# Two small transfers of 64 query weight rows, over eight DMA engines, for the second and third group

## The chip, the core and the metric

The kernel runs on one core of a Trainium2 chip. The metric is the time of one execution on the device in microseconds, the median of several runs. A profile is one further execution with the hardware profiler on; its rows are quoted as the profile prints them.

## The reference

One decode step of a block with attention over cached keys and values and an MLP, for 4 sequences, in float32:

```python
# B=4, D=448, 16 query heads on 8 key heads, Dh=256, window W=1024 of the cache
q = layernorm(x) @ wq                        # wq: 448 x 4096
scores = einsum("bhqd,bhkd->bhqk", q, k[-W:]) * Dh ** -0.5
o = einsum("bhqk,bhkd->bhqd", softmax(scores), v[-W:])
h = x + o @ wo                               # wo: 4096 x 448
y = layernorm(h)
out = h + gelu(y @ w1 + b1) @ w2 + b2        # F = 1792
```

About 88 MB of keys, values and weights are read once. The work per byte is small.

## The kernel before, in words

**Groups.** The 8 key heads are 8 groups, 0 to 7. A group has two query heads and needs its part of the query weights wq (448 rows x 512 columns), keys, values and a part of wo. For each group TensorE projects the queries (`project_q`, line 152, with a transposition at 158), multiplies them with the keys in two halves (`scores_half`, line 172), transposes the probabilities (line 204), multiplies with the values (`values`, line 216) and adds the group's share of the output (`add_output`, line 245). VectorE takes maxima, scales and copies; ScalarE copies and takes exponentials. The MLP follows at the end, with w1 at line 443 and w2 at lines 469 (`pa`) and 479 (`py`).

**Loads.** All loads are issued by the sync engine SP, in the order of the program, through `load` (line 58) into three ring slots of 128 rows (tag `r`). Slot `t0` takes wq of group 0 with x and biases (`wq0`) and then the keys of group 0 with the first 384 rows of group 1's wq (`k0`). Four kinds of ring load follow, twice: `ta` (from `la`), `tb` (`lb`), `tc` (`lc`) and `td` (`ld`), for three groups each time, 14080 or 15872 words a row. The last loads go into the slots `te`: keys and values of the last groups, w1 and w2. w2 comes in four pieces, the last of which has 448 words a row. A ring slot is loaded again as soon as its readers are done; SP waits for them. The order on TensorE, ScalarE and SP is that of the program text.

**The query weights.** 448 is three times 128 and a rest of 64 rows. `wq_parts` (line 70) lists a group's products. Rows 0 to 383 are three products of 128 rows x 512 columns. The rest is usually packed on the host as 128 rows x 256 columns, the left half of the columns above the right half, and needs two products of 256 columns: `yT[:, 3]` has the normalised x in its upper 64 rows and zeros below, `yT[:, 4]` the other way round. Group 1 is the exception: its rest comes as plain 64 rows x 512 columns in a small tile of its own, `wq1_last`, and is one product. That tile is loaded by two transfers at line 265, between `k0` and the first ring load. Their source has an outer dimension of 8, with a gap of 512 words behind each eighth, and each fills 32 rows of the tile.

In the names of the views `wq_last<-wq` is that small load, `pq` a projection, `s` scores, `po` the product with the values. `yT`, `project_q(g, ...)` and the loop `for g in (0, 3)`, which handles groups g+1 to g+3, are what the change touches.

Of the kernel before, what the change touches and what calls it, by code (L numbers as in the profile page):

```python
# [8 lines left out]
F32 = mybir.dt.float32  # L9
# [6 lines left out]
B, D = 4, 448  # L16
HQ, HKV, SK, DH = 16, 8, 4096, 256
# [3 lines left out]
P = 128  # L21
H = P // 2
# [4 lines left out]
Q = 32  # L27
CACHE = NKC * B * DH
HALF = CACHE // 2
WEIGHTS = 4 * D  # L30
# [3 lines left out]
SCALE = DH ** -0.5  # L34

@with_exitstack
def block_kernel(ctx: ExitStack, tc, wq0, k0, wq1, la, lb, lc, ld, k7, vo, w1, w2, out):
    nc = tc.nc
    const = ctx.enter_context(tc.tile_pool(name="const", bufs=1))
    ring = ctx.enter_context(tc.tile_pool(name="ring", bufs=3))  # L40
    work = ctx.enter_context(tc.tile_pool(name="work", bufs=2))
# [9 lines left out]
    def slot(name):  # L51
        return ring.tile([P, SLOT], F32, tag="r", name=name)

    def load(t, at, src, pieces=None):
        dst = t[:, at : at + src.shape[-1]]
        at = 0
        for n in pieces or (src.shape[-1],):
            nc.sync.dma_start(dst[:, at : at + n], src[:, at : at + n])  # L58
            at += n
        return dst  # L60

    def cut(t, sizes):
        parts, at = [], 0
        for n in sizes:
            parts.append(t[:, at : at + n])
            at += n
        return parts


    def wq_parts(t, last=None):  # L70
        parts = [(a, yT[:, a, :], slice(0, 512), t[:, a * 512 : (a + 1) * 512]) for a in range(3)]
        if last is not None:
            return parts + [(3, yT[:H, 3, :], slice(0, 512), last)]
        for i in range(2):
            parts.append((3, yT[:, 3 + i, :], slice(i * 2 * P, (i + 1) * 2 * P), t[:, 3 * 512 :]))
        return parts


    def keys(t):
        return t.rearrange("p (c b k) -> p c b k", c=2, b=B)  # L80

    def chunks(t):
        v = t.rearrange("p (c b d) -> p c b d", b=B, d=DH)
        return [v[:, c : c + 2] for c in range(0, v.shape[1], 2)]
# [17 lines left out]

    yT = const.tile([P, ND + 1, Q], F32, name="yT")
    nc.vector.memset(yT, 0.0)
    wq1_last = const.tile([H, 512], F32, name="wq1_last")
    zT = const.tile([P, ND, Q], F32, name="zT")
    nc.vector.memset(zT, 0.0)

# [40 lines left out]
    def project_q(g, parts):  # L149
        pq = ps_m.tile([P, 512], F32, tag="m", name=f"pq{g}")  # L150
        for j, y, cols, w in parts:
            nc.tensor.matmul(pq[j * Q : (j + 1) * Q, cols], y, w, start=True, stop=True)  # L152
        qs = work.tile([P, 512], F32, tag="qs", name=f"qs{g}")
        nc.scalar.copy(qs, pq)  # L154

        pt = ps_m.tile([P, 2 * REP, P], F32, tag="m", name=f"pqt{g}")
        for i in range(2 * REP):
            nc.tensor.transpose(pt[:, i, :], qs[:, i * P : (i + 1) * P], ident)  # L158
        sm = work.tile([P, 2 * REP, B], F32, tag="sm", name=f"sm{g}")
        nc.vector.tensor_reduce(  # L160
            sm, pt.rearrange("p i (j q) -> p i q j", j=4)[:, :, :B, :], axis=AX.X, op=ALU.add
        )

        src = sm.rearrange("p (r c) b -> p c b r", r=REP)
        for i in range(2):
            nc.vector.tensor_copy(qT[g % 2][:, :, :, i * REP : (i + 1) * REP], src)
# [13 lines left out]
    def softmax(g, parts):  # L180
        halves, mx = zip(*parts)
        nm = work.tile([P, 1], F32, tag="nm", name=f"nm{g}")
        nc.vector.tensor_max(nm, mx[0], mx[1])
        nc.vector.tensor_scalar_mul(nm, nm, -SCALE)  # L184
        p = once.tile([P, 2 * 512], F32, tag="p", name=f"p{g}")
        sums = work.tile([P, 2], F32, tag="sums", name=f"sums{g}")
        for h in range(2):
            nc.scalar.activation(  # L188
                p[:, h * 512 : (h + 1) * 512], halves[h], AF.Exp, bias=nm, scale=SCALE,
                accum_out=sums[:, h : h + 1],  # L190
            )
        rec = work.tile([P, 1], F32, tag=f"rec{g % 3}", name=f"rec{g}")
        nc.vector.tensor_add(rec, sums[:, 0:1], sums[:, 1:2])
        nc.vector.reciprocal(rec, rec)
        return p, rec

    def scores(g, kt):
        return [scores_half(g, h, kt[h]) for h in range(2)]

    def transpose_p(g, p):  # L200
        for h in range(2):
            pt = ps_t.tile([P, 4, P], F32, tag="t", name=f"ppt{g}_{h}")
            for c in range(4):
                nc.tensor.transpose(pt[:, c, :], p[:, (4 * h + c) * P : (4 * h + c + 1) * P], ident)  # L204

            src = pt.rearrange("p (c i) (b q) -> p c i b q", i=2, b=B)
            for i in range(2):
                nc.vector.tensor_copy(  # L208
                    pT[g % 2][:, 2 * h : 2 * h + 2, :, i * REP : (i + 1) * REP], src[:, :, i, :, :REP]
                )  # L210


    def values(g, vt, po, pairs=range(NKC // 2)):
        for c in pairs:
            for b in range(B):
                nc.tensor.matmul(  # L216
                    po[b * Q : (b + 1) * Q], pT[g % 2][:, c, b, :], vt[c][:, :, b, :],
                    start=(c == 0), stop=(c == NKC // 2 - 1),
                )
# [35 lines left out]
    def po_tile(g, pool=ps_o, tag="o"):  # L255
        return pool.tile([P, 2, DH], F32, tag=tag, name=f"po{g}")


    t = slot("t0")
    wqt, xT, b2T, b1T = cut(load(t, 0, wq0), (WEIGHTS, ND * B, 4, 4 * 4))  # L260
    wqt = wq_parts(wqt)
    xT = xT.rearrange("p (a b) -> p a b", a=ND)
    ka, kb, wqt1 = cut(load(t, WEIGHTS + COLUMNS, k0), (HALF, HALF, 3 * 512))
    for i in range(2):
        nc.sync.dma_start(  # L265
            wq1_last[i * Q : (i + 1) * Q, :], wq1[i].rearrange("e (p c) -> e p c", c=512)[:, :4, :]
        )
    d = work.tile([P, ND, B], F32, tag="d", name="d_x")
    centred(d, xT, "x")
    sx = work.tile([P, ND, B], F32, tag="sx", name="sx")  # L270
# [20 lines left out]
        nc.scalar.copy(rs[:, at : at + cols], pr.rearrange("p i c -> p (i c)")[:, :cols])  # L291

    parts = scores(0, [keys(ka), keys(kb)])
    project_q(1, wq_parts(wqt1, wq1_last))
    p, rec = softmax(0, parts)
    transpose_p(0, p)

    def finish(g, po, rec, wt):
        transposed_output(g, po, rec)
        add_output(g, output_weights(wt))  # L300

    for g in (0, 3):
        ka, kb, wqt, va = cut(load(slot(f"ta{g}"), 0, la[g // 3]), (HALF, HALF, WEIGHTS, HALF))
        parts = scores(g + 1, [keys(ka), keys(kb)])
        project_q(g + 2, wq_parts(wqt))
        p, rec_next = softmax(g + 1, parts)
        transpose_p(g + 1, p)
        po = po_tile(g)
        va = chunks(va)
        values(g, va, po, range(0, 2))  # L310

        vb, wot, ka, kb = cut(load(slot(f"tb{g}"), 0, lb[g // 3]), (HALF, WEIGHTS, HALF, HALF))
        values(g, va + chunks(vb), po, range(2, 4))
        p, rec_then = softmax(g + 2, scores(g + 2, [keys(ka), keys(kb)]))
        finish(g, po, rec, wot)
        transpose_p(g + 2, p)

        wqt, v, wot, ka = cut(load(slot(f"tc{g}"), 0, lc[g // 3]), (WEIGHTS, CACHE, WEIGHTS, HALF))
        project_q(g + 3, wq_parts(wqt))
        po = po_tile(g + 1)  # L320
        values(g + 1, chunks(v), po)
        first_half = scores_half(g + 3, 0, keys(ka))
        finish(g + 1, po, rec_next, wot)

        kb, wqt, v, wot = cut(load(slot(f"td{g}"), 0, ld[g // 3]), (HALF, WEIGHTS, CACHE, WEIGHTS))
        parts = [first_half, scores_half(g + 3, 1, keys(kb))]
        project_q(g + 4, wq_parts(wqt))
        p, rec = softmax(g + 3, parts)
        transpose_p(g + 3, p)
        po = po_tile(g + 2)  # L330
        values(g + 2, chunks(v), po)
        finish(g + 2, po, rec_then, wot)


    g = HKV - 2
    e = [slot(f"te{i}") for i in range(3)]
# [7 lines left out]
    p, rec_last = softmax(g + 1, scores(g + 1, kt))  # L344
# [27 lines left out]
    last = ps_s.tile([P, 512], F32, tag="s", name="last")[:, :P]  # L372
# [102 lines left out]
    for c in range(first, NFC):  # L475
        for j in range(4):
            m, n = (Q, 2) if c == first else (B, 2 if j < 3 else 1)
# [79 lines left out]
```

## Time and profile before

| | |
|---|---|
| median of 3 runs | 213.85 us (213.79 to 213.94) |
| profiled execution | 214.16 us |
| its span, first to last instruction | 212.4 us |
| DMA engines, queue of the loads | 96.9% of 16 engines' span |
| TensorE busy | 133.9 us (63%) |
| VectorE, ScalarE busy | 39.0 us, 22.1 us |
| read from HBM | 88.23 MB |

A line of the busy list gives engine, busy time, share of the span and number of instructions. In rows of groups and of the timeline stand line, engine, operation and tiles, written from read, and in brackets how long the engine had been idle and what ended that. SP's rows are the issues of transfers. In rows of stretches stand start and end, length, busy time of PE (matmul), PEld (weight load), DVE (VectorE), ACT (ScalarE) and POOL (GpSimd), each with its number of instructions, then the clock granted to TensorE, the mean share of the 16 DMA engines that is busy, and GB/s. A DMA row of a queue has packets, MB and share. The chain of waits is followed back from the last instruction.

### The profile page before, as it was taken

Reading aid. Unit: us, or ns where it says so; the run is one execution under the profiler, and the core shown is the slowest. Engines: PE = TensorE matmul, PEld = TensorE weight load, DVE = VectorE, ACT = ScalarE, POOL = GpSimd, SP = SyncE. Lnnn points to the kernel's source line nnn. Section 1 sums busy time; section 2 is a strip of 40 time slices with the busy share of each in tenths; the row PEclk is TensorE's granted clock in tenths of the full one; section 3 lists DMA queues with packets and bytes.
Section 4 is the critical chain, followed back from the end, with each engine's and each line's share of the span. In section 5 each row is a group of like instructions: output and inputs, shape, how many; then the busy total and the mean of one; then the engine's idle time right before and its main releaser. Section 6 shows DMA issues by size and latency. Waiting matters only on the chain.

```text
span 212.4 us, 2302 instructions
## 1 busy us (share of the span) xinstructions
PE 133.9 (63%) x976; PEld 48.3 (23%) x976; DVE 39.0 (18%) x170; ACT 22.1 (10%) x54; POOL 5.0 (2%) x16
## 2 busy tenths in 40 slices
PE   0469805843950696288398098138708879978984
PEld 0342201310220221022123023013202323224432
DVE  1520300410230003022013013100301223112310
ACT  2011300300020100030003002001000302010311
POOL 5100000000000000000000000000000000000200
PEclk9999995995896559589969759856985999999999
DMA  7999898999999999999999999999989999999991
GB/s 294 425 396 534 361 488 361 491 394 475 407 395 529 395 407 430 451 403 459 424 424 488 403 395 505 395 430 419 478 350 460 430 429 394 440 400 444 419 384 52
DMA packets 3257, 88.43 MB, mean 416 GB/s; under 512 B 368, under 2 KB 624, under 8 KB 1328
## 3 DMA queue, kind: packets, MB, share of 16 engines
q1 hardware_dynamic: 3248, 88.30, 96.9%
q8 instruction: 7, 0.11, 0.2%
q14 instruction: 2, 0.02, 0.0%
HBM read 88.23 MB, written 0.07 MB: 416 GB/s over the span
## 4 chain that ended last, share of the span: by engine, by line
DMA 78%; PE 16%; SPq 2%; DVE 1%; issue 1%; ACT 1%; ACTq 0%
DMA tb<-lb 22%; DMA ta<-la 21%; DMA td<-ld 20%; DMA te<-w 14%; PE s L172 6%; PE po L216 4%; SPq L58 2%; PE ppt L204 1%; PE pq L152 1%; PE acc L245 1%; PE pa L469 1%; PE py L479 1%; SPq L265 1%; PE pqt L158 1%; ACT qs L154 1%
## 5 line engine op out<-in xcount | busy, mean ns | idle before, releaser
L177 DVE TENSOR_REDUCE mx<-s 128x1 f32<-128x512 f32 x16 | 11.1, 691 | 57.8 <-PE s L172 57.8
L172 PE MATMUL s<-ta,qT 128*32 128x512 f32 x64 | 10.7, 831 | 10.3 <-DMA ta<-la 10.3
L154 ACT COPY qs<-pq 128x512 f32<-128x512 f32 x8 | 4.7, 585 | 113.3 <-PE pq L152 113.3
L188 ACT ACTIVATE p<-s,nm 128x512 f32<-128x512 f32 x16 | 10.9, 687 | 46.1 <-DVE nm L184 46.1
L233 DVE TENSOR_SCALAR o<-po,rec 128x512 f32<-128x512 f32 x8 | 6.0, 750 | 48.5 <-PE po L216 48.5
L216 PE MATMUL po<-tb,pT 128*32 128x512 f32 x32 | 7.2, 1051 | 12.2 <-DMA tb<-lb 12.2
L172 PE MATMUL s<-td,qT 128*32 128x512 f32 x32 | 7.1, 1042 | 12.1 <-DMA td<-ld 12.1
L152 PE MATMUL pq<-tc,yT 128*32 128x512 f32 (+1 forms) x20 | 3.9, 891 | 16.6 <-DMA tc<-lc 16.6
L204 PE MATMUL ppt<-ident,p 128*128 128x128 f32 x64 | 10.5, 287 | 0.7 <-ACT p L188 0.4
L216 PE MATMUL po<-tc,pT 128*32 128x512 f32 x64 | 10.4, 813 | 0.0
L158 PE MATMUL pqt<-ident,qs 128*128 128x128 f32 x32 | 6.6, 341 | 6.0 <-ACT qs L154 6.0
L204 PEld LDWEIGHTS ppt<-ident,p 128*128 128x128 f32 x64 | 6.7, 141 | 6.3 <-ACT p L188 6.3
L160 DVE TENSOR_REDUCE sm<-pqt 128x16 f32<-128x64 f32 x8 | 1.8, 224 | 34.4 <-PE pqt L158 34.4
L216 PE MATMUL po<-te,pT 128*32 128x512 f32 x64 | 7.5, 595 | 0.5 <-DMA te<-vo 0.5
L172 PE MATMUL s<-tb,qT 128*32 128x512 f32 x64 | 7.4, 607 | 0.0
L216 PE MATMUL po<-td,pT 128*32 128x512 f32 x64 | 7.3, 595 | 0.0
L237 PE MATMUL pot<-ident,o 128*128 128x128 f32 x32 | 5.2, 286 | 2.7 <-DVE o L233 2.7
L158 PEld LDWEIGHTS pqt<-ident,qs 128*128 128x128 f32 x32 | 4.2, 169 | 11.4 <-ACT qs L154 9.7
L351 PE MATMUL warm<-idle 128*32 128x512 bf16 x22 | 6.8, 382 | 0.0
L172 PEld LDWEIGHTS s<-ta,qT 128*32 128x32 f32 x64 | 2.6, 148 | 17.7 <-issue 13.7
L208 DVE COPY pT<-ppt 128x16 f32<-128x16 f32 x32 | 4.7, 171 | 7.6 <-PE ppt L204 7.6
L172 PE MATMUL s<-t,qT 128*32 128x512 f32 x32 | 5.4, 833 | 0.5 <-DMA t<-k 0.5
(134 smaller groups left out, 112.4 us busy)
## 6 DMA issues: line engine op xcount, KB each, us to landing
tc<-lc SPq DMA_DIRECT2D x2, 7936.0 KB, 47.0
td<-ld SPq DMA_DIRECT2D x2, 7936.0 KB, 44.0
ta<-la SPq DMA_DIRECT2D x2, 7040.0 KB, 38.1
tb<-lb SPq DMA_DIRECT2D x2, 7040.0 KB, 43.2
te<-vo SPq DMA_DIRECT2D x1, 4992.0 KB, 28.1
t<-k SPq DMA_DIRECT2D x1, 4864.0 KB, 15.8
te<-k SPq DMA_DIRECT2D x1, 4096.0 KB, 37.8
te<-vo SPq DMA_DIRECT2D x1, 3072.0 KB, 14.8
```

The source lines that it names most:

```text
L152: nc.tensor.matmul(pq[j * Q : (j + 1) * Q, cols], y, w, start=True, stop=True)
L154: nc.scalar.copy(qs, pq)
L158: nc.tensor.transpose(pt[:, i, :], qs[:, i * P : (i + 1) * P], ident)
L172: nc.tensor.matmul(s[b * Q : (b + 1) * Q, :], qT[g % 2][:, c, b, :], kt[:, c, b, :], start=(c == 0), stop=(c == 1),)
L177: nc.vector.reduce_max(m, s, axis=AX.X)
L188: nc.scalar.activation(p[:, h * 512 : (h + 1) * 512], halves[h], AF.Exp, bias=nm, scale=SCALE, accum_out=sums[:, h : h + 1],)
L204: nc.tensor.transpose(pt[:, c, :], p[:, (4 * h + c) * P : (4 * h + c + 1) * P], ident)
L208: nc.vector.tensor_copy(pT[g % 2][:, 2 * h : 2 * h + 2, :, i * REP : (i + 1) * REP], src[:, :, i, :, :REP])
L216: nc.tensor.matmul(po[b * Q : (b + 1) * Q], pT[g % 2][:, c, b, :], vt[c][:, :, b, :], start=(c == 0), stop=(c == NKC // 2 - 1),)
L233: nc.vector.tensor_scalar_mul(o, po, rec)
L237: nc.tensor.transpose(pt[:, i, c], o[:, i, c * P : (c + 1) * P], ident)
L351: nc.tensor.matmul(warm[:Q], idle[:, :Q], idle, start=True, stop=True)
```

## The change

The tile `wq1_last` (64 rows) becomes `wq_last` (128 rows): group 1's rest lies in rows 0 to 63, group 2's in rows 64 to 127. The two transfers stand at the same place in SP's order, and each now brings 64 rows of 512 words. The source again has an outer dimension of 8 and a gap behind each eighth. The first ring load no longer holds group 2's rest and has 256 words a row less; for that `la` becomes two tensors, `la0` and `la1`. Group 2's projection has one product of 64 rows x 512 columns, with `yT[H:, 4]` as its other side. Groups 3 to 7 are as before.

```diff
-    wq1_last = const.tile([H, 512], F32, name="wq1_last")
+    wq_last = const.tile([P, 512], F32, name="wq_last")
...
     for i in range(2):
-        nc.sync.dma_start(
-            wq1_last[i * Q : (i + 1) * Q, :], wq1[i].rearrange("e (p c) -> e p c", c=512)[:, :4, :]
-        )
+        nc.sync.dma_start(wq_last[i * H : (i + 1) * H], wq_rest[i].rearrange("e (p c) -> e p c", c=512)[:, :8, :])
...
         if last is not None:
-            return parts + [(3, yT[:H, 3, :], slice(0, 512), last)]
+            return parts + [(3, last[0], slice(0, 512), last[1])]
...
-    project_q(1, wq_parts(wqt1, wq1_last))
+    project_q(1, wq_parts(wqt1, (yT[:H, 3, :], wq_last[:H])))
...
     for g in (0, 3):
-        ka, kb, wqt, va = cut(load(slot(f"ta{g}"), 0, la[g // 3]), (HALF, HALF, WEIGHTS, HALF))
+        n = WEIGHTS if g else 3 * 512
+        ka, kb, wqt, va = cut(load(slot(f"ta{g}"), 0, la[g // 3]), (HALF, HALF, n, HALF))
         parts = scores(g + 1, [keys(ka), keys(kb)])
-        project_q(g + 2, wq_parts(wqt))
+        project_q(g + 2, wq_parts(wqt, None if g else (yT[H:, 4, :], wq_last[H:])))
...
-    la = np.concatenate([k[1:5:3], wq[2:6:3], va[0:4:3]], axis=2)
+    la0 = np.concatenate([k[1], wq[2][:, : 3 * 512], va[0]], axis=1)
+    la1 = np.concatenate([k[4], wq[5], va[3]], axis=1)
...
-    wq1 = np.asarray(A_wq).reshape(D, HKV, 512)[3 * P :, 1].reshape(2, 8, 4 * 512)
-    wq1 = np.concatenate([wq1, np.zeros((2, 8, 512), np.float32)], axis=2)
+    wq_rest = np.asarray(A_wq).reshape(D, HKV, 512)[3 * P :, 1:3].transpose(1, 0, 2).reshape(2, 8, 8 * 512)
+    wq_rest = np.concatenate([wq_rest, np.zeros((2, 8, 512), np.float32)], axis=2)
```

On SP's queue at the start of the program the transfers stood like this (written from read, rows x words):

```order
L58 DMA t_129<-wq 128x1828
L58 DMA t_129<-k 128x9728
L265 DMA wq_last<-wq 32x1x512 x2
L58 DMA ta_247<-la 128x14080
L58 DMA tb_321<-lb 128x14080
L58 DMA tc_390<-lc 128x15872
```

Now they are these:

```order
L59 DMA t_129<-wq 128x1828
L59 DMA t_129<-k 128x9728
L266 DMA wq_last<-wq_rest 64x1x512 x2
L59 DMA ta_247<-la 128x13824
L59 DMA tb_320<-lb 128x14080
L59 DMA tc_389<-lc 128x15872
```

The order is the same; the small transfers have twice the rows, and the first ring load is 256 words narrower.

On TensorE the scores of group 1 and the projection of group 2 (`pq_271`), which follow the first ring load, were these:

```order
L172 MATMUL s_1_260<-ta_247,qT_112 32x512 x8
L152 MATMUL pq_271<-ta_247,yT 32x512 x3
L152 MATMUL pq_271<-ta_247,yT 32x256 x2
L158 MATMUL pqt_279<-ident,qs_277 128x128 x4
L204 MATMUL ppt_0_298<-ident,p_291 128x128 x4
```

They are now:

```order
L173 MATMUL s_1_260<-ta_247,qT_112 32x512 x8
L153 MATMUL pq_271<-ta_247,yT 32x512 x3
L153 MATMUL pq_271<-wq_last,yT 32x512
L159 MATMUL pqt_278<-ident,qs_276 128x128 x4
L205 MATMUL ppt_0_297<-ident,p_290 128x128 x4
```

The two products of 256 columns from the ring slot are one of 512 columns from the small tile; nothing else moves.

More of the change, by code (lines that the diff above doesn't have):

```diff
@@ L36, in block_kernel @@
 @with_exitstack
-def block_kernel(ctx: ExitStack, tc, wq0, k0, wq1, la, lb, lc, ld, k7, vo, w1, w2, out):
+def block_kernel(ctx: ExitStack, tc, wq0, k0, wq_rest, la0, la1, lb, lc, ld, k7, vo, w1, w2, out):
     nc = tc.nc
+    la = (la0, la1)
     const = ctx.enter_context(tc.tile_pool(name="const", bufs=1))
@@ L541 @@
     arrays = {
-        "wq0": np.concatenate([wq[0], xT, b2, b1], axis=1), "k0": k0, "wq1": wq1, "la": la, "lb": lb, "lc": lc, "ld": ld, "k7": k[7], "vo": vo, "w1": w1, "w2": w2,
+        "wq0": np.concatenate([wq[0], xT, b2, b1], axis=1), "k0": k0, "wq_rest": wq_rest, "la0": la0, "la1": la1, "lb": lb, "lc": lc, "ld": ld, "k7": k[7], "vo": vo, "w1": w1, "w2": w2,
     }
```

## The prediction

> **What bounds the kernel now.** I read the page's engine shares and chain first, then the time table by stretches, then the wait table of the DMA-issuing queue and the timeline of the tail. The page says who is busy:
>
> ```profile
> span 212.4 us, 2302 instructions
> PE 133.9 (63%) x976; PEld 48.3 (23%) x976; DVE 39.0 (18%) x170; ACT 22.1 (10%) x54; POOL 5.0 (2%) x16
> ...
> q1 hardware_dynamic: 3248, 88.30, 96.9%
> q8 instruction: 7, 0.11, 0.2%
> ...
> DMA 78%; PE 16%; SPq 2%; DVE 1%; issue 1%; ACT 1%; ACTq 0%
> ```
>
> The 16 DMA engines are taken for 96.9% of the span and TensorE for 63%. The table by stretches (length, busy time of PE, PEld, DVE, ACT, POOL, the PE clock, DMA share, GB/s) shows the load stream itself and its last half microsecond:
>
> ```profile
> 17.40:200.00 182.60, 118.50 (x840) 40.11 (x836) 32.05 (x133) 17.80 (x45) 0.48 (x1) 0.83 1.00 429
> 208.20:208.70 0.50, 0.50 (x19) 0.21 (x16) 0.00 (x0) 0.16 (x1) 0.00 (x0) 1.00 0.06 22
> 208.70:209.20 0.50, 0.50 (x24) 0.27 (x16) 0.00 (x0) 0.00 (x0) 0.00 (x0) 1.00 0.00 0
> ```
>
> From 17.4 to 200 us the share is 1.00: no engine pauses, at 429 / 16 = 26.8 GB/s each. So the end is a sum of bytes, engine by engine, and it is the sum of the engine that ends last. Between 208.2 and 208.7 the share is 0.06, one sixteenth: a single engine still works, 0.06 x 16 x 0.5 = 0.48 us of that half microsecond, so it ends at 208.68 while the other fifteen are through by 208.2. The tail hangs on it:
>
> ```profile
> 206.00 1.71 PE L469 MATMUL pa<-te,gT 128*32 128x448 f32 x16 [0.69 <-DMA te<-w]
> ...
> 209.20 0.11 PEld L479 LDWEIGHTS py<-te,gT 128*4 128x4 f32 x8 [0.23 <-DMA te<-w]
> 209.67 0.29 DVE L485 TENSOR_TENSOR res<-py,hb 128x128 f32<-128x128 f32 x1 [4.42 <-PE py L479]
> ```
>
> The first product with w2 waited 0.69 us for its piece, and the last weights at 209.20 waited again, for the last piece. What moves the last landing later moves the end by as much; what moves it earlier gains until something else is late.
>
> **The change, part by part.** The sum is made against the profiled execution, 214.16 us, which is its span of 212.4 and 1.76 around it; the median of the runs shown, 213.85, lies 0.31 lower, and I carry the same difference over to it.
>
> *Bytes per engine.* Before, two transfers of 32 rows x 2 KB = 64 KB go over eight engines, 8 KB on each of them per transfer. Now they are 64 rows x 2 KB = 128 KB, 16 KB on each of the eight per transfer. So each of the eight carries 2 x 8 KB = 16 KB more, 16384 / 26.8 = 0.61 us at the pace above. The first ring load is narrower by 256 words, 256 x 4 B x 128 rows = 128 KB, over sixteen engines 8 KB or 0.31 us less on each. Net at full pace: the eight +0.30 to +0.31, the other eight -0.31. No byte is saved. Which engines the eight are, no view here shows; I assume the same eight for both transfers, before and now. [...]
>
> *Is the last engine one of the eight?* They already carry 16 KB more than the others (two transfers of 8 KB), so they run 0.61 us behind them from the start of the ring; the other disturbances are seven instruction packets of 0.11 MB / 7 = 16 KB, which can fall on any engine. I take 8 in 10 for one of the eight.
>
> *Rows that are filled from two sides.* Before, the two transfers filled rows 0 to 31 and 32 to 63. Now the second fills rows 64 to 127, while the other eight engines already stream the ring load, which covers all 128 rows. If the pace of 26.8 GB/s is that of an engine, nothing is added. If it is that of the path into a group of rows, two engines on one group go at half pace. In every ring stage each engine has its own share of the rows, so no row of before tells these apart. Bounds, in units of 16 KB on each of eight engines (0.61 us): nothing at the low end; at the other end, the second transfer in turns with one ring engine costs 0.61 more, in turns with a ring engine and a second one of the eight 1.22, and the first transfer, if its engines pair up on the same rows (eight rows each now, four before), another 0.61. That is 0 to 1.83. I take sharing as likelier than not, since the stretch of 429 GB/s with share 1.00 holds loads of 14080 and of 15872 words a row alike, which speaks for a path of fixed width rather than a cost per piece, and of its range 0.61 to 1.83 the middle, 1.22.
>
> [...]
>
> *TensorE and the wait for the rows.* Group 2's projection replaces two products of 128 rows x 256 columns by one of 64 rows x 512. The rows by line (min/median/max ns, first and last start), and the waits:
>
> ```profile
> L152 PE MATMUL pq<-ta,yT x20: 379/592/592, 39.3 to 111.8; 128*32 128x512 f32 x12, 128*32 128x256 f32 x8
> ...
> L152 PE MATMUL pq<-wq_last,yT x2: 589/601/613, 23.3 to 23.7; 64*32 64x512 f32 x2
> ```
>
> ```profile
> PE po L216 <- DMA tb<-lb: 12.2, 2, 6.4
> ...
> PE s L172 <- DMA ta<-la: 10.3, 2, 7.1
> ```
>
> A product has two records. Of the ten in group 2, two of 256 columns go and the last two become 64 x 512 at 601 ns, like group 1's now: no more work than before, and behind it TensorE waits up to 6.4 us for the second ring load anyway. Cost 0; if that cover were gone, some tenths. The rows that group 2 uses from the small tile must have landed; they are ahead of its ring load in the same queue, so nothing new is waited for. Group 1 used its rows at 23.3:
>
> ```profile
> 1.62 1.55 SPq L265 DMA_DIRECT2D wq_last<-wq  x2
> 3.21 0.47 SPq L58 DMA_DIRECT2D ta<-la  x1
> 3.73 0.44 SPq L58 DMA_DIRECT2D tb<-lb  x1
> 23.40 0.33 SPq L58 DMA_DIRECT2D tc<-lc  x1
> ```
>
> ```profile
> 17.14 5.36 PE L172 MATMUL s<-t,qT 128*32 128x512 f32 x32 [0.50 <-DMA t<-k]
> ...
> 23.28 1.04 PE L152 MATMUL pq<-wq_last,yT 64*32 64x512 f32 x2
> ...
> 34.13 5.40 PE L172 MATMUL s<-ta,qT 128*32 128x512 f32 x32 [7.12 <-DMA ta<-la]
> ```
>
> ```profile
> 51.45 3.56 PE po L216 x16
> ...
> 60.57 45.35 DMA ta<-la
> ```
>
> ```profile
> ta<-la SPq DMA_DIRECT2D x2, 7040.0 KB, 38.1
> ```
>
> The load of k0 landed at 17.1 and the small transfers lie right behind it; even 2 x 0.61 + 1.83 = 3.05 us after it is 20.2, ahead of 23.28. Cost 0, with 3 us of cover. The next two rows are of the chain: values wait at 51.45 for the second ring load, and the load that carries the chain on from 60.57 takes 45.35 us from its issue; the last row is its size.
>
> *The issuing queue.* SP needs 1.55 us for the two small transfers; with twice the rows at most 3.1, since a transfer can cost no more than in proportion. Then the first ring load is issued at 4.8 instead of 3.21, and the engines are busy with k0 until about 17: hidden behind 12 us. The later ring loads are issued when TensorE lets go of a slot, tc at 23.40, which is 11 us before its predecessor tb begins to move (ta landed at 34.1). The chain shows the same distance later: 45.35 us from issue to landing for 7040 KB, which move in 7.21 MB / 429 GB/s = 16.8 us, so such a load lies 28 us in the queue before it moves. A stream that is later by 2 us leaves that as it is.
>
> *Sum, likeliest case.* Eight engines: +0.31 (0.61 more, 0.31 less, rounded) + 1.22 from sharing = +1.53, between 0.31 + 0.61 = 0.92 and 0.31 + 1.83 = 2.14. All of it passes to the last landing and, as the tail waits there, to the end: 214.16 + 1.53 = 215.69 profiled, 213.85 + 1.53 = **215.4 us**. The other eight would be late by 0.61 - 0.31 = 0.30 and are not last. If the last engine is one of these others, the eight overtake it under sharing: from at most 208.2 to at most 209.7, up to 1.05 us behind the 208.68 of before.
>
> **The rivals.**
>
> *Full pace.* The rows take what two engines bring, and the eight are later by 0.31 alone: 213.85 + 0.31 = 214.16 us for the median, 0.14% over before. For it: every row of before shows an engine's pace and none a slowdown. Against it: that engines on the same rows never met there.
>
> *The end is not on the eight.* Then, at full pace, the last engine is relieved by 0.31 and ends at 208.37, while the eight move from at most 208.2 to at most 208.51: the end comes 0.17 to 0.31 sooner. It can be more where the instruction packets decide who is last; one falls late:
>
> ```profile
> q1 hardware_dynamic: 61, 0.59, 94.7%
> q8 instruction: 1, 0.02, 4.5%
> ```
>
> That is the stretch 202.5 to 204. Should it strike an engine that has time in the changed program, the lone 0.48 us goes too: 0.31 + 0.48 = 0.79 at most. Middle 0.48, 213.37 us. It decides from the point at which the last engine belongs to those that the change unloads, and only if shared rows cost less than 0.31. For it: the others would then be the ones with more instruction packets. Against it: the 0.61 us by which the eight start behind.
>
> That the change does not do what it says would mean sixteen engines for the small transfers: 256 KB / 16 = 16 KB on each, as the eight carry today, and 8 KB less in the ring load: -0.31 for the eight, +0.30 for the others. The source's outer size of 8 is the same as before, so I give it no chance of its own.
>
> **How the numbers follow.** A measurement of this kernel can tell about 0.2% from no change, 0.43 us: the line lies at 213.42 and 214.28. Sharing 0.58, all of it slower (its own range 214.8 to 216.0). Full pace 0.24: at +0.31 mostly within, 0.18, and 0.06 slower, should rows of 2 KB cost a little more than their bytes. End not on the eight 0.18: its range -0.17 to -0.79 is cut at -0.43, 0.11 faster, 0.07 within. Slower 0.58 + 0.06 = 0.64, same 0.18 + 0.07 = 0.25, faster 0.11. The predicted time is that of sharing. The range goes up to its upper bound, 213.85 + 2.14 = 216.0, and down into the third case to 213.6, which leaves out about 0.13 below and 0.05 above.
>
> **What would show it.** The first product of the first ring load, at 34.13 now, starts later by what the eight lost: about 35.7 under sharing, 34.4 at full pace. The same shift should stand at 51.45, where the second ring load is awaited, and at the first product with w2, 206.00. A shift that is there at 34.13 but not at 206.00 would say that the last engine is not one of the eight. TensorE's group 2 projection should show eight records instead of ten, with its wait for the next load still behind it, and group 1's small rows no wait. I am wrong if the ring starts later by 1 us and more and the end does not, or if the end moves with no shift at 34.13.

## The result and the profile after

The changed kernel takes 215.57 us (median of 6 runs, 215.49 to 215.67) against 213.94 us of the kernel before in runs beside it: 1.63 us more, a ratio of 1.0077 with a 95% interval of 1.0064 to 1.0090. Its profiled execution took 215.63 us.

The page of the changed kernel shows the same share for the loads and no more bytes; TensorE is busy 2.8 us longer, but the shares of the chain are the same:

```profile
span 213.8 us, 2297 instructions
PE 136.7 (64%) x974; PEld 48.5 (23%) x974; DVE 39.1 (18%) x170; ACT 22.1 (10%) x54; POOL 5.0 (2%) x16
...
q1 hardware_dynamic: 3312, 88.30, 96.9%
q8 instruction: 7, 0.11, 0.2%
...
DMA 78%; PE 16%; SPq 2%; DVE 1%; issue 1%; ACT 1%; ACTq 0%
```

The queue has 64 packets more (the added small rows) and the same 88.30 MB. Its timeline shows TensorE at the places that the prediction named: the small rows of group 1, the first ring load, the projection of group 2, the second ring load.

```profile
24.32 1.04 PE L153 MATMUL pq<-wq_last,yT 64*32 64x512 f32 x2
...
35.65 5.48 PE L173 MATMUL s<-ta,qT 128*32 128x512 f32 x32 [7.61 <-DMA ta<-la]
40.95 1.04 PE L153 MATMUL pq<-ta,yT 128*32 128x512 f32 x6
41.92 1.04 PE L153 MATMUL pq<-wq_last,yT 64*32 64x512 f32 x2
...
53.04 3.61 PE L217 MATMUL po<-tb,pT 128*32 128x512 f32 x16 [5.48 <-DMA tb<-lb]
```

The first product of the first ring load starts at 35.65 where it started at 34.13: 1.52 us late. At the second ring load it is 53.04 against 51.45, 1.59 late. So the loss is there when the first ring load lands, and it is still there at the end:

```profile
207.47 1.71 PE L469 MATMUL pa<-te,gT 128*32 128x448 f32 x16 [0.23 <-DMA te<-w]
...
210.64 0.11 PEld L479 LDWEIGHTS py<-te,gT 128*4 128x4 f32 x8 [0.20 <-DMA te<-w]
211.12 0.29 DVE L485 TENSOR_TENSOR res<-py,hb 128x128 f32<-128x128 f32 x1 [3.94 <-PE py L479]
```

The first product with w2 starts 1.47 later, the wait for its last piece ends 1.44 later (209.20 before). In between the shift is not constant: the scores that wait for the second load `td` start at 161.32 against 160.10, 1.22 late.

The table by stretches shows where the time is lost. In it the four microseconds after k0 are, in the kernel before,

```profile
16.00:20.00 4.00, 3.50 (x19) 1.14 (x22) 0.00 (x0) 0.72 (x2) 0.00 (x0) 1.00 1.13 483
```

and in the changed kernel

```profile
16.00:20.00 4.00, 3.27 (x16) 1.08 (x18) 0.06 (x1) 0.88 (x2) 0.00 (x0) 1.00 1.24 397
```

The last two numbers are the DMA share and GB/s. (Both count a packet whole near one end of a short stretch, so a share can pass 1; their quotient is what counts.) The engines are as occupied as before and deliver less: 483 / 1.13 = 427 GB/s per full share, about the 429 of the whole stream, falls to 397 / 1.24 = 320. Packets take longer; none are missing.

The kept trace has every packet's time and shows it directly. In the kernel before, each small row (2048 bytes) takes 84 ns and each engine's first row of the first ring load (56320 bytes) 2079 ns. In the changed kernel the small rows begin at the same time (15.98 us, 16.00 before), but they take up to 264 ns, about three times as long, and the last of them ends at 18.21 us where it ended at 16.91. The first ring row of every one of the sixteen engines is slower too: 3133 to 3229 ns on the eight that have no small rows and 2521 to 2752 ns on the eight that have them, where such a row (now 55296 bytes) takes 2042 to 2056 ns once the small rows are through.

### The profile page after: what moved, and what is told of

It is laid out like the page before. It is cut to its first block, busy times and chain, and to the rows that moved or that the text cites. A ratio compares the mean times of both kernels' runs of the same rounds, so it can differ in the third digit from the quotient of the medians.

```text
span 213.8 us, 2297 instructions
## 1 busy us (share of the span) xinstructions
PE 136.7 (64%) x974; PEld 48.5 (23%) x974; DVE 39.1 (18%) x170; ACT 22.1 (10%) x54; POOL 5.0 (2%) x16
## 3 DMA queue, kind: packets, MB, share of 16 engines
q1 hardware_dynamic: 3312, 88.30, 96.9%
## 4 chain that ended last, share of the span: by engine, by line
DMA 78%; PE 16%; SPq 2%; DVE 1%; issue 1%; ACT 1%; ACTq 0%
DMA tb<-lb 23%; DMA ta<-la 21%; DMA td<-ld 20%; DMA te<-w 14%; PE s L173 6%; PE po L217 4%; SPq L59 2%; PE ppt L205 1%; PE pq L153 1%; PE acc L246 1%; PE pa L469 1%; PE py L479 1%; SPq L266 1%; PE pqt L159 1%; ACT qs L155 1%
## 5 line engine op out<-in xcount | busy, mean ns | idle before, releaser
L173 PE MATMUL s<-t,qT 128*32 128x512 f32 x32 | 6.0, 920 | 0.7 <-DMA t<-k 0.7
```

The source lines that it names most:

```text
L173: nc.tensor.matmul(s[b * Q : (b + 1) * Q, :], qT[g % 2][:, c, b, :], kt[:, c, b, :], start=(c == 0), stop=(c == 1),)
```

## The experiments

The theory that was forecast: engines that fill the same rows at the same time share one way into them. The rivals: only the bytes of the eight engines count (+0.31), or many small rows on eight engines cost by themselves, wherever they go. The diffs below show the transfers alone, without the packing on the host and the products that follow them. Two measures are used for each kernel: the start of the first product of the first ring load, against 34.13 (a shift inside one execution), and the median against that of the kernel before in the same call.

**Same bytes, same eight engines, rows 0 to 63 only, four rows an engine.** Group 2's rest goes to a free corner of the first ring slot.

```diff
-    for i in range(2):
-        nc.sync.dma_start(wq_last[i * H : (i + 1) * H], wq_rest[i].rearrange("e (p c) -> e p c", c=512)[:, :8, :])
+    ta0 = slot("ta0")
+    wq_last2 = ta0[:H, SLOT - 512 :]
+    for i in range(4):
+        nc.sync.dma_start(
+            (wq_last, wq_last2)[i // 2][i % 2 * Q : (i % 2 + 1) * Q],
+            wq_rest[i].rearrange("e (p c) -> e p c", c=512)[:, :4, :],
+        )
...
```

> The same bytes on the same eight engines as in the changed kernel (32 KB each ahead of the first ring load, which stays 256 words narrower), but in four transfers of 32 rows, all into rows 0 to 63, four rows an engine as before: group 2's rest lies in a free corner of the first ring slot. Shared rows: no two engines meet on the same rows, so only the bytes are left, +0.31 us over before, 214.2 to 214.3. Rival, a cost of many small rows on eight engines wherever they go: as the changed kernel, 215.6.

Measured: 214.43 against 213.81 us, ratio 1.0028 (1.0018 to 1.0039), +0.62. Its first product of the first ring load and its stretch after k0:

```profile
34.46 6.54 PE L173 MATMUL s<-ta,qT 128*32 128x512 f32 x32 [7.89 <-DMA ta<-la]
```

```profile
16.00:20.00 4.00, 3.56 (x19) 1.10 (x21) 0.00 (x0) 0.68 (x2) 0.00 (x0) 1.00 1.16 493
```

The ring starts 0.33 late, which is the price of the bytes (0.31 forecast), and the quotient is 493 / 1.16 = 425 GB/s, unchanged. In the trace of this kernel all 128 small rows take 84 ns, and the first ring rows 2041 ns. So neither the number of small rows nor the load of the eight engines explains 1.52: it must be where the rows lie, or how many of them an engine takes in one transfer. The median moved by more than the start, 0.62; that is taken up below.

**Group 2's rest in rows 64 to 127, but four rows an engine.**

```diff
-    for i in range(2):
-        nc.sync.dma_start(wq_last[i * H : (i + 1) * H], wq_rest[i].rearrange("e (p c) -> e p c", c=512)[:, :8, :])
+    for i in range(4):
+        nc.sync.dma_start(wq_last[i * Q : (i + 1) * Q], wq_rest[i].rearrange("e (p c) -> e p c", c=512)[:, :4, :])
...
```

> As the changed kernel, with group 2's rest in rows 64 to 127, but in four transfers of 32 rows, four rows an engine. Shared rows: the first two transfers are free of it, the other two meet one ring engine each on their rows and go at half pace: +0.31 + 0.61 = +0.92 us over before, 214.8 to 214.9, with the first ring load's start shifted by as much. Rival, small rows on eight engines: as the changed kernel, 215.6. If only the number of rows that an engine takes in one transfer counted (eight against four): +0.31, 214.25.

Measured: 215.00 us, ratio 1.0066 (1.0047 to 1.0085), +1.19. The product starts here:

```profile
34.90 5.50 PE L173 MATMUL s<-ta,qT 128*32 128x512 f32 x32 [9.05 <-DMA ta<-la]
```

That is +0.77. Against the kernel of rows 0 to 63 only the destination of the same pieces differs (and the half of `yT` that the product reads), and it costs 0.77 - 0.33 = 0.44 at the start, 215.00 - 214.43 = 0.57 in the medians. The stretch after k0 has the lower pace, 475 / 1.25 = 380 GB/s:

```profile
16.00:20.00 4.00, 3.53 (x28) 1.35 (x30) 0.35 (x2) 0.86 (x2) 0.00 (x0) 1.00 1.25 475
```

In the trace the small rows now take up to 175 ns, about twice 84, and the first ring rows of the other eight engines 2540 to 2582 ns. So rows 64 to 127 beside the ring load cost 0.44 us at the start with four rows an engine, less than the 0.61 of full turns and less than half of the whole 1.52.

**The kernel before with group 1's rest as one transfer of 64 rows.**

```diff
-    for i in range(2):
-        nc.sync.dma_start(
-            wq1_last[i * Q : (i + 1) * Q, :], wq1[i].rearrange("e (p c) -> e p c", c=512)[:, :4, :]
-        )
+    nc.sync.dma_start(wq1_last, wq1.rearrange("e (p c) -> e p c", c=512)[:, :8, :])
...
```

> The kernel before, with group 1's rest as one transfer of 64 rows (eight rows an engine, rows 0 to 63) in place of two of 32: the same bytes on the same engines. Shared rows: two of the eight engines meet on the same rows and take turns, at most +0.61 us, 214.5; this is the first of the three parts of the sharing that was forecast. Rival, that only the meeting with the ring load's engines costs: no change, 213.9.

Measured: 214.23 us, ratio 1.0021 (1.0013 to 1.0030), +0.42. The start:

```profile
34.30 5.81 PE L172 MATMUL s<-ta,qT 128*32 128x512 f32 x32 [8.36 <-DMA ta<-la]
```

+0.17, with the same bytes on the same engines into the same 64 rows. Eight rows an engine in place of four cost something, as pairs on the same rows would, but at the start less than a third of the 0.61 that was given as the most. The trace does not show pairs alone: the small rows take up to 194 ns, but the first ring rows of all sixteen engines are slower as well, 2255 to 2413 ns.

**Both rests as one transfer of 128 rows over sixteen engines.**

```diff
-    for i in range(2):
-        nc.sync.dma_start(wq_last[i * H : (i + 1) * H], wq_rest[i].rearrange("e (p c) -> e p c", c=512)[:, :8, :])
+    nc.sync.dma_start(wq_last, wq_rest)
...
```

> The rests of both groups as one transfer of 128 rows over all sixteen engines: 16 KB on each, where before the eight carried 16 KB and the others none; the ring load is 256 words narrower as in the changed kernel. The eight are relieved by 0.31, the others take 0.31 more, no engine meets another on its rows. If the engine that ends last is one of the eight: 0.17 to 0.31 us sooner than before, 213.6 to 213.8. If it is one of the others: +0.31, 214.25. If the cost in the changed kernel came from the products or the order on TensorE, which are its own here: 215.6.

Measured: 214.10 us, ratio 1.0016 (1.0007 to 1.0025), +0.29. The start:

```profile
34.16 5.86 PE L173 MATMUL s<-ta,qT 128*32 128x512 f32 x32 [8.36 <-DMA ta<-la]
```

The narrower ring load, the tile of 128 rows and group 2's product of 64 rows are all in this kernel, and the 1.6 us are not: TensorE has no part in the loss. But the end came later, not sooner. That agrees with the branch "one of the others" and speaks against the assumption that the eight alone decide the end. All small rows take 84 ns here as well.

**Only group 2's rest as a transfer of 64 rows.** Group 1's comes in two of 32 rows again.

```diff
+    for i in range(2):
+        nc.sync.dma_start(wq_last[i * Q : (i + 1) * Q], wq1[i].rearrange("e (p c) -> e p c", c=512)[:, :4, :])
+    nc.sync.dma_start(wq_last[H:], wq_rest.rearrange("e (p c) -> e p c", c=512)[:, :8, :])
...
```

> The changed kernel with group 1's rest in two transfers of 32 rows as before and only group 2's as one transfer of 64 rows into rows 64 to 127. Measured so far, as the shift of the first product of the first ring load against 34.13: bytes alone +0.33, one transfer of 64 rows for group 1 +0.17, group 2 in rows 64 to 127 by four rows an engine +0.77, the changed kernel +1.52. If the three parts of the sharing add up, taking group 1's pairs away leaves 1.52 - 0.17 = 1.35, 215.4 us. Rival, that the cost needs both wide transfers together: near +0.77, 214.9.

Measured: 215.37 against 213.94 us, ratio 1.0069 (1.0056 to 1.0081), +1.43. The start:

```profile
35.47 5.21 PE L173 MATMUL s<-ta,qT 128*32 128x512 f32 x32 [9.71 <-DMA ta<-la]
```

+1.34 where 1.35 was expected from the sum of the parts: the wide first transfer is worth 0.18 here and 0.17 alone. The medians say 1.63 - 1.43 = 0.20 here and 0.42 alone, so the parts add up less well than the starts alone suggest. The second transfer makes up nearly everything.

**Both transfers of 64 rows, both into rows 0 to 63.**

```diff
-    for i in range(2):
-        nc.sync.dma_start(wq_last[i * H : (i + 1) * H], wq_rest[i].rearrange("e (p c) -> e p c", c=512)[:, :8, :])
+    ta0 = slot("ta0")
+    wq_last2 = ta0[:H, SLOT - 512 :]
+    for i in range(2):
+        nc.sync.dma_start((wq_last, wq_last2)[i], wq_rest[i].rearrange("e (p c) -> e p c", c=512)[:, :8, :])
...
```

> The changed kernel with its two transfers of 64 rows, eight rows an engine, but both into rows 0 to 63 (group 2's in a free corner of the first ring slot), where the other eight engines do not write. Sharing: bytes +0.33 and two transfers with pairs, 2 x 0.17, so the ring starts +0.67 later, 214.7 us. Rival, that eight rows an engine cost by themselves and the meeting with the ring load does not: as the changed kernel, +1.52, 215.5.

Measured: 214.91 us, ratio 1.0044 (1.0032 to 1.0057), +0.97. The start:

```profile
35.06 5.79 PE L173 MATMUL s<-ta,qT 128*32 128x512 f32 x32 [8.78 <-DMA ta<-la]
```

+0.93, between the two expectations. This kernel and the changed one differ in the place that the second transfer fills (and the half of `yT` that goes with it), and the difference is 1.52 - 0.93 = 0.59 us at the start, 0.66 in the shifts of the medians: about one unit of 16 KB on each engine at full pace (0.61), which is what half pace in the meeting with one ring engine comes to. The corner of the ring slot costs nothing by itself, since four rows an engine went into it at full pace. The rest, 0.93 - 0.33 = 0.60 (0.35 in the medians), belongs to eight rows an engine in two transfers, 0.17 for the first and so 0.43 for the second. Why the second costs more than the first is open.

The expectation took it that the other eight engines do not write into rows 0 to 63, so that only pairs within a transfer would be left. The stretch after k0 does not bear that out, at 479 / 1.26 = 380 GB/s, as slow as with rows 64 to 127 in fours:

```profile
16.00:20.00 4.00, 3.30 (x24) 1.14 (x26) 0.00 (x0) 0.76 (x2) 0.00 (x0) 1.00 1.26 479
```

In the trace the first ring rows of the other eight engines take 2474 to 2535 ns here too. So a transfer of eight rows an engine slows engines that carry none of its rows, even when it stays in rows 0 to 63, and the split into a meeting of 0.59 and pairs of 0.60 is one of conditions, not of mechanisms.

The kernels side by side (shifts in us, pace as GB/s per full share between 16 and 20 us, longest small row and first ring rows in ns from the traces; at full pace a ring row takes 2079 ns before and with group 1 as one of 64 rows, 2041 in the others, which are 256 words narrower):

| kernel | start | median | pace | small row | first ring row, other eight engines | the eight |
|---|---|---|---|---|---|---|
| before | 0 | 0 | 427 | 84 | 2079 | 2079 |
| sixteen engines | +0.03 | +0.29 | 427 | 84 | 2041 | - |
| rows 0 to 63, four an engine | +0.33 | +0.62 | 425 | 84 | 2041 | 2041 |
| group 1 as one of 64 rows | +0.17 | +0.42 | 407 | 194 | 2255 to 2413 | in the same range |
| rows 64 to 127, four an engine | +0.77 | +1.19 | 380 | 175 | 2540 to 2582 | 2335 to 2535 |
| two of 64 rows, rows 0 to 63 | +0.93 | +0.97 | 380 | 164 | 2474 to 2535 | 2239 to 2353 |
| only group 2 as one of 64 rows | +1.34 | +1.43 | 339 | 253 | 2900 to 3024 | 2439 to 2891 |
| changed kernel | +1.52 | +1.63 | 320 | 264 | 3133 to 3229 | 2521 to 2752 |

**The kernel before, a second profiled execution.**

> The kernel before, unchanged, for a second profiled execution: the first one took 214.16 us where the runs beside it took 213.6 to 214.0. If that execution was drawn out by instruction packets on the engine that ends last, this one shows no engine alone behind the others in the last half microsecond and ends about 0.3 us sooner, with the first ring load's product at the same 34.1. Otherwise it repeats the first.

Measured: ratio 1.0003 (0.9993 to 1.0012); the profiled execution took 214.00 us against 214.16 of the first. The start is the same, the end is not. The timeline and the last stretches of this second execution:

```profile
34.09 5.24 PE L172 MATMUL s<-ta,qT 128*32 128x512 f32 x32 [7.18 <-DMA ta<-la]
...
209.06 0.11 PEld L479 LDWEIGHTS py<-te,gT 128*4 128x4 f32 x8 [0.23 <-DMA te<-w]
```

```profile
208.00:208.50 0.50, 0.50 (x19) 0.16 (x9) 0.00 (x0) 0.20 (x1) 0.00 (x0) 1.00 0.31 118
208.50:209.00 0.50, 0.50 (x24) 0.32 (x16) 0.00 (x0) 0.00 (x0) 0.00 (x0) 1.00 0.00 0
```

The share of 0.31 is five engines on average between 208.0 and 208.5, and none after. The first execution had 0.11 there and 0.02 after: a single straggler, whose last piece lands 0.48 us behind the next engine's (0.06 in the second execution). So the lone engine belonged to that execution. It is no rarity: the kernel of rows 0 to 63 also ends on one engine, whose last piece lands 0.82 us behind the next.

```profile
208.50:209.00 0.50, 0.49 (x20) 0.21 (x15) 0.00 (x0) 0.18 (x1) 0.00 (x0) 1.00 0.06 22
```

Which engine that is, and whether an instruction packet made it late, no view says.

## Why the prediction was right

Forecast were 215.4 us and a range of 213.6 to 216.0; measured 215.57.

*The sharing of rows.* This was the likeliest case, +1.53. Its place and its two conditions are shown: packets go slower while the small rows are written, and they do so when the rows are 64 to 127 beside the running ring load (380 GB/s per full share against 427) or when an engine takes eight of them in one transfer (407), and not for the bytes or the number of small rows (425) or TensorE. The ring starts at 35.65 (35.7 forecast). Of the 1.52 us, 0.33 are bytes (0.31 forecast) and 1.19 slower packets (1.22 taken, the middle of 0.61 to 1.83). The parts are not thirds as the bounds had them. Rows 64 to 127 cost 0.59 with eight rows an engine and 0.44 with four (0.61 forecast). Eight rows an engine cost 0.43 in the second transfer (0.61) and 0.17 to 0.18 in the first (0.61). That the middle fitted so well is therefore partly luck.

*What the forecast mis-sized* is the delay of the other eight engines. It had them late by 0.61 - 0.31 = 0.30, one turn of 16 KB less the narrower load. In the trace their first ring row takes 1.09 to 1.19 us longer than at full pace, nearly two turns, so they are late by about 0.8. That is the size of three engines taking turns, which the forecast had as an estimate in its upper bound. It does not explain why they are slower by 0.43 to 0.49 us when both transfers stay in rows 0 to 63; what holds up the packets there stays open.

The 0.59 between the two kernels that differ in rows 64 to 127 (35.65 against 35.06) agrees with two engines that take turns on one way. Pairs within a transfer of eight rows an engine agree in sign with the costs of 0.17 and 0.43, which fall short of full turns, and such pairs do not account for the slower ring rows of the other eight engines. No view names the engine of a row or a way into it, so the ways, the pairs and the turns of 0.61 remain the author's estimate; the runs show what each condition costs, not by which mechanism. Another cause in the wide transfers, such as the eight rows that lie in one piece in the source, was not tested apart from it.

*The same eight engines for both transfers* was an assumption. The trace of the changed kernel agrees with it: eight engines go from their last row of k0 straight to their first ring row, at 16.14 to 16.78 us, while the small rows run on to 18.21; the other eight begin theirs at 17.80 to 18.21.

*Full pace* is refuted as the case that happened, but its price is measured: the kernel with the same bytes in rows 0 to 63 starts the ring 0.33 late. *The end not on the eight* did not decide the sign, yet it held a truth that the forecast's main line missed.

*The step that was wrong* is "8 in 10 for one of the eight", together with the lone straggler read from one execution and the 0.61 us by which the eight were to start behind. The second execution has no straggler. In the trace of the kernel before the eight begin their first ring row at 16.65 to 16.91 us, the others at 16.00 to 16.65: about 0.3 us behind (medians 16.81 and 16.51), because the others finish k0 later (their last rows of it end at 16.00 to 16.65, those of the eight at 16.00 to 16.26). Relieving the eight and loading the others (sixteen engines) costs 0.29; loading the eight and relieving the others (rows 0 to 63) costs 0.62. Both directions lose, which fits two halves that end nearly level in the kernel before; that the second loses 0.62 where the bytes give at most 0.31 is not explained. It did no harm here because, by the fallback in the sum, a shift of 1.5 us puts the eight last in either case. For a change of 0.3 us it would have decided.

The first profiled execution of the kernel before also ended late, though not beyond its kind: 214.16 us, with 213.63 to 213.97 in 25 later runs and 213.73 to 214.20 in 25 more after those. Against it the shift of the end is 1.44; against the runs it is 1.63. The 0.31 that was carried over as a constant fits the straggler, which was 0.48 behind; the second execution, at 214.00, lies 0.06 above the median of the runs beside it.

*What was costed at nothing* stayed there: group 2's projection has eight records (40.95 and 41.92) and a wait of 5.48 us for the next load behind it; group 1's rows are read at 24.32 with no wait.

None of the kernels tried beats the one before, whose two transfers of 32 rows slow no packet (84 ns a small row, 2079 a ring row).

## What to carry to other kernels

Here a load that was meant to balance the DMA engines had to be laid out for the rows it fills as well. Four rows an engine in rows 0 to 63 went at full pace (84 ns a row) beside the next large load, which had already begun on the other engines; the same pieces in rows 64 to 127 (up to 175 ns), or eight rows an engine (164 to 264 ns at the longest), did not. In this stream, which is full from start to end, a loss of 1.52 us at its head was still there, with 1.44, at the last wait. But a single wait does not give its size. The kernel with sixteen engines is late by 0.03 us at the first ring load, 0.79 at the second and 0.29 in the medians, and two executions of the kernel before differ by 0.04 at the first and 0.28 at the second. The size is read from the medians, the place from the first wait. Who is last at the end should be read from more than one execution.

## What was not expected of the hardware

Twice the rows did not cost the issuing queue more time: the two small transfers took SP 1.55 us with 32 rows each and 1.40 us with 64, where in proportion to the rows it would have been 3.1.

```profile
1.64 1.40 SPq L266 DMA_DIRECT2D wq_last<-wq_rest  x2
3.08 0.48 SPq L59 DMA_DIRECT2D ta<-la  x1
```

The first ring load is issued at 3.08, even sooner than at 3.21. Four transfers of 32 rows instead took 2.98 us in the kernel with rows 64 to 127, so in these runs the number of transfers counts, not their rows.
